# Retention and a normed two-layer block on one core: the norm's gain folded into w1, x of tiles 8 on normalized by ScalarE, and two more units of the first product built from seven half-size products

## The chip, the cores and the metric

The kernel runs on one core of a Trainium2 chip. The metric is the device time of one execution in microseconds (us). TensorE is called PE here as in the profile's rows (PEld is its weight loads), VectorE DVE, ScalarE ACT, GpSimd POOL and SyncE SP. Three runs of the kernel before are given, and one more execution that was profiled.

## What is computed

Inputs q, k and v have the shape 4 x 8 x 768 x 64 (batch, heads, sequence, head width). For each head a decaying state runs along the sequence; then a norm over the 512 features, a product with w1 (512 x 2048), a maximum with zero, a product with w2 (2048 x 512), and the sum with the input of the norm:

```python
gamma = 1.0 - 2.0 ** (-5.0 - np.arange(H))
state = gamma * state + k[t] (x) v[t]            # for t = 0 .. 767, each batch and head
y[t]  = scale * q[t] @ state
x  = y as [4, 768, 512]
mu, var = mean and variance of x over its 512 features
xn = (x - mu) / np.sqrt(var + 1e-06) * g_ln
out = x + np.maximum(xn @ w_ch1, 0.0) @ w_ch2
```

## The kernel before

**Tiles.** The 4 x 768 positions are 24 tiles of 128: tiles 0 to 3 are the first of each batch, then come five of batch 0 (4 to 8), five of batch 1, and so on. Everything between the loads and the store of the result stays on chip, and the state is carried between tiles of a batch as a sum in the PSUM bank PD.

**The order is written out by hand.** The string ORDER (lines 31 to 99) is a list of tokens. The loop at its end (lines 787 to 790) emits them one after the other, so an engine works through its own instructions in the order of the tokens, and an engine that waits for one token holds back all its later ones. A token is a name with numbers, then the engine where there is a choice (A is ACT, D DVE, S SP), then the PSUM banks that it uses (X0 to X3, Y0, Y1, M, PD). With the tile t the tokens are:

- `k`, `q`, `v` load a tile (line 355), issued by POOL; `gk`, `gq`, `gv` are POOL's waits for a landed load's buffer (line 384); `vg` is POOL's product of v with decay factors (line 475). `tr` transposes q and k of a tile from 7 on by a DMA issued by SP (line 398), `eq` scales q on DVE (line 404).
- `vis` (lines 407 to 422) is a visit of one tile, from tile 8 on of a pair of tiles: products of k and q into X banks, and the state's part of y into the banks Y0 and Y1. `am` is the mask on DVE (line 426), `py` adds the rest of y in Y0 and Y1 (line 441), `pd` adds to the state's sum in PD (line 483), and `pb` writes the next state out of PD, with ACT (line 494, four instructions) or DVE (line 498, two).
- Of a finished y: `bn` (lines 449 and 450, DVE) has mean and variance, `xc` (line 465, ACT) keeps x as bf16 for the end. `xn` (line 459, DVE) is (y - mean) times g; the row g is spread over the partitions by a matmul into `gb`. Up to tile 9 `xn` goes straight to the bf16 tile xn, and the factor 1/sqrt(var) is left to the end: `sq` and `rs` make it for a group, and `ad` (line 566, DVE) multiplies the second product by it and adds x. From tile 10 on (S0) `xn` goes to a float32 buffer (arg or grow), `sr` (line 577, ACT, square root) and `rt` (line 581, DVE, reciprocal) make the factor for the tile, and `xg` (line 585, ACT) multiplies by it into the bf16 tile. From tile 7 on y lies in Y0 and Y1 by halves (even and odd heads), so `xn` and `xc` come as a and b.
- `ex` brings xn transposed into xnt; from tile 8 (TX) on that is a DMA issued by SP (line 518).
- `m` (line 543) is a unit of the first product: 16 matmuls of 128 columns for a tile, or 8 of 256 columns for a group of two tiles, or 4 of 512 columns for a group of four; `r` (line 554 ACT or 556 DVE) takes the maximum with zero into h1. Tiles 0 to 7 are groups of one, 8 to 15 groups of two (groups 8 to 11), 16 to 19 and 20 to 23 groups of four (12 and 13).
- Six of the eight units of groups 12 and 13 (`seven` in line 18) use seven products of half the size in place of eight: `f` (line 646) has 4 matmuls of 256 columns; `fs` (line 657, ACT) copies a partial product out, `fo` (line 667, DVE) and `fq` (line 672, ACT) form the blocks of h1, `fr` (line 681 ACT or 679 DVE) takes the maximum with zero. `wm` (line 613, and 608 for number 3) and `xt` (line 629) make the sums of weights and of x, on DVE.
- `z` (line 561) is the second product up to tile 9. From tile 10 on it too goes by seven half-size products for a pair of tiles: `sa` (line 695, DVE) sums, `s` (line 706) 8 matmuls of 256 columns, `o` (line 720, DVE) additions that end in the output tile; `tm` (line 595) makes the sums of w2. `st` (line 573) stores, issued by ACT.

A visit writes Y0 and Y1, so it can't write y before `bn`, `xn` and `xc` of the visit before have read them.

Of the kernel before, what the change touches and what calls it, by code (L numbers as in the profile page):

```python
# [17 lines left out]
 'seven': [(12, 2), (12, 3), (13, 0), (13, 1), (13, 2), (13, 3)],  # L18
# [46 lines left out]
gq18 xg14 v19 rt15 vis16//X0,X1,X2,X3 ad9 st4/A ex14/S gq16 pd17 vg3/ am17a s10_1//M pb18/A am16a
tr18 m10_14//X2 v18 sa10_2 st7/A m10_12//X0 gk19 am16b v20 st5/A am17b pd3 gq19 m10_4//X1 tm3 pb19/A
tr19 py16 py17 m10_0//X3 sa10_4 r10_4/A xg15 bn17 m10_6//X1 xc16a ex15/S xc16b bn16 s10_5 r10_14/A
gv18 v21 xc17a tr20 sr17 s10_2//X2 xn17b r10_0/A gv19 rt17 k21 xn16a sr16 r10_6/A m10_2//X3 xn17a
o10_1 xc17b gk20 vg19/ xg17 m10_10//X1 rt16 o10_2 r10_12/A ex17/S q21 r10_2/A s10_6 eq18 xn16b
r10_10/A sa10_3 v22 s10_3 st6/A eq19 vis18//X0,X1,X2,X3 o10_3 o10_4 pd19 am19a s10_7 pb20/A gk21  # L70
am18a m10_8//X2 q22 o10_5 am18b s10_4 k22 r10_8/A am19b xg16 py18 sa12_1 q23 py19 st8/A m11_14//X0
ex16/S o10_6 gv20 bn19 vg20/ m11_2//X1 tr21 bn18 sr19 gq21 s12_1//M vg21/ xc19a xc19b wm1 m11_4//X2
sr18 vg22/ r11_14/A xc18a m11_6//X3 xc18b rt18 k23 xn19a r11_2/A rt19 s12_5 xn19b r11_6/A v23 xn18b
xg19 xn18a m11_10//X0 sa12_2 r11_4/A ex19/S xg18 pd20 o12_1 m11_0//X1 pb21/A wm2 ex18/S s12_2//X2
r11_0/A eq20 m11_8//X3 tr22 r11_10/A o12_2 eq21 s12_6 r11_8/A sa12_4 vis20//X0,X1,X2,X3 sa12_3 pd21
s12_3 am21a pb22/A am20b m11_12//X2 am21b m12_9//X1 am20a wm4 py20 r12_9/A py21 m12_0//X0 bn20
m12_1//X1 r12_0/A bn21 r11_12/A pd22 m12_10//X0 xc20a r12_1/A o12_3 m12_3//X2 pb23/A xn20a tr23
xt12_1 o12_4 m12_11//X1 xn21b sr20 xn21a xc20b s12_7 rt20 sr21 sa14_1 xc21a r12_10/A m12_2//X3 rt21
xn20b r12_3/A eq22 s14_1//PD o12_5 r12_2/A eq23 r12_11/A s12_4 wm3 xc21b st12/A vis22//X0,X1,X2,X3
st10/A xg21 xt12_2 s14_5 o12_6 xg20 am23b ex20/S f12_3_1//M am22a m12_8//X3 am22b st9/A ex21/S  # L80
fs12_3_1 f12_3_2//X0 am23a st11/A f12_3_5//X1 sa14_2 f12_3_6 fs12_3_5 fo12_3_1 f12_2_1//X2 r12_8/A
py22 xt12_3 f12_3_3 fs12_2_1 xt12_4 f12_2_5//X0 fs12_3_2 o14_1 f12_2_6 fs12_2_5 sa14_4 f12_3_7
fs12_2_2 py23 fo12_3_2 f12_2_3 f12_2_7 fo12_3_3 fr12_3_1/A s14_6 bn23 f13_1_1//X1 xc23b fo12_2_3
f12_3_4 xc22a f12_2_2//X3 fo12_2_2 fq12_3 f12_2_4 fo12_2_1 xc23a s14_2//X0 sr23 fq12_2 xn23b
fr12_2_1/A bn22 f13_1_2//X3 s14_3 fr12_2_2/A xn23a f13_0_1//X2 rt23 sr22 sa16_1 xc22b s16_1//M xg23
xn22a fr12_3_2/A rt22 ex23/S xn22b s16_5 o14_3 xg22 sa14_3 f13_0_2//Y0 ex22/S o14_4 s16_2//Y1 sa16_2
s14_7 o16_1 o14_2 s16_6 o14_5 st14/A sa16_4 fs13_0_1 s14_4 fs13_1_1 o16_2 sa16_3 f13_3_1//X0
f13_2_1//Y1 xt13_1 o14_6 s16_3 xt13_2 fo13_1_1 f13_0_5//PD fo13_0_1 f13_1_6 fs13_0_5 f13_0_6 sa18_1
fs13_3_1 f13_3_5//X3 xt13_3 fs13_1_2 f13_1_5//Y0 o16_3 fs13_0_2 f13_0_3 sa18_2 st15/A f13_3_6
fo13_0_2 fs13_2_1 f13_0_7 fs13_1_5 f13_1_7 o16_4 f13_2_6 fr13_0_1/A fo13_1_3 f13_3_2//PD xt13_4  # L90
s16_7 fs13_2_2 fo13_0_3 st13/A f13_1_3 fo13_3_1 f13_2_7 fo13_1_2 f13_1_4 fr13_1_2/D s18_1//PD
fs13_3_2 o16_5 fs13_3_5 f13_0_4 fq13_1 f13_3_7 fq13_0 f13_3_3 fo13_3_3 f13_2_5//X1 fo13_3_2
f13_2_2//X2 fs13_2_5 s18_5 sa18_4 fr13_3_1/A fo13_2_3 f13_3_4 f13_2_3 fr13_3_2/D fo13_2_1 s16_4
# [9 lines left out]
def kernel(  # L103
# [10 lines left out]
    nc = tc.nc  # L114
# [87 lines left out]
    xhat = [arg.rearrange("p i t -> p (i t)"), grow]  # L202
# [253 lines left out]
    @on("xn")  # L456
    def _(eng, t, half):
        dst, src, g = y_parts(t, half, slot(xns if t < S0 else xhat, t))
        nc.vector.scalar_tensor_tensor(out=dst, in0=src, scalar=mv[:, t, 0:1], in1=g,  # L459
                                       op0=ALU.subtract, op1=ALU.mult)  # L460
# [117 lines left out]

    @on("rt")
    def _(eng, t):  # L580
        nc.vector.reciprocal(out=rstd[:, t:t + 1], in_=rstd[:, t:t + 1])

    @on("xg")
    def _(eng, t):
        nc.scalar.activation(out=slot(xns, t), in_=slot(xhat, t), func=AF.Copy, scale=rstd[:, t:t + 1])
# [235 lines left out]
```

## Time and profile before

| | us |
|---|---|
| median of three runs | 206.64 (206.2 to 208.77) |
| the profiled execution | 205.83 |
| span from its first to its last instruction | 204.1 |
| PE, PEld busy | 195.7, 153.7 |
| DVE, ACT, POOL busy | 164.9, 103.0, 98.2 |

Granted TensorE clock: 0.996 over the span. The span leaves 1.7 us of the profiled execution outside. A row that groups instructions gives line, engine, operation, tiles written and read, shapes and count, then the time in which at least one of them ran and the mean duration of one; as neighbours overlap, the first divided by the count is less than the mean.

### The profile page before, as it was taken

To read this page: it belongs to the slowest core of one execution; us is meant where nothing else is said; L and a number is where in the kernel's file an instruction comes from. 1 tells how busy PE (TensorE), PEld (TensorE's weight loads), DVE (VectorE), ACT (ScalarE), POOL (GpSimd) and SP (SyncE) were. 2 spreads that over 40 slices of the span, in tenths; PEclk is the share of its full clock that TensorE was granted. 3 is DMA by queue.
4 is the path that set the end of the run, shared out by engine and by line. 5 is a ranking of instruction groups with operands and counts; after the bars stand their busy time and mean duration, and the time that the engine had idled before them with its cause. 6 is when DMAs were issued, how large, how long until landed. Compare 5 with 4: busy or idle time off the path is not lost.

```text
span 204.1 us, 5621 instructions
## 1 busy us (share of the span) xinstructions
PE 195.7 (96%) x2255; PEld 153.7 (75%) x2255; DVE 164.9 (81%) x380; ACT 103.0 (50%) x241; POOL 98.2 (48%) x145
## 2 busy tenths in 40 slices
PE   7988999999999999999999999999999999999992
PEld 2548899898645766668586988876579888888881
DVE  6677889769247879689398989999999899789871
ACT  5363654551331815926557684773967854641000
POOL 8986786496397599667298355960000000000000
PEclk9999999999999999999999999999999999999998
DMA  9999999999999999999999999999052031102025
GB/s 129 168 183 179 158 194 169 149 169 170 139 136 168 135 142 134 137 160 152 172 156 145 207 185 172 163 111 145 3 184 78 0 103 51 55 0 106 0 104 206
DMA packets 109949, 27.14 MB, mean 133 GB/s; under 512 B 102626, under 2 KB 106978, under 8 KB 109923
## 3 DMA queue, kind: packets, MB, share of 16 engines
q0 software_dynamic: 77024, 13.37, 92.7%
q1 hardware_dynamic: 28242, 6.85, 24.9%
q10 hardware_dynamic: 4656, 6.56, 10.5%
q8 instruction: 17, 0.28, 0.6%
q14 instruction: 10, 0.07, 0.1%
HBM read 27.30 MB, written 6.29 MB: 165 GB/s over the span
## 4 chain that ended last, share of the span: by engine, by line
PE 51%; DMA 27%; POOL 12%; issue 6%; DVE 2%; ACT 1%; POOLq 0%; ACTq 0%
PE X L543 16%; DMA v<-in_v_dram 11%; PE X L646 6%; DMA qk<-in_k_dram 6%; PE Y L706 6%; PE PD L706 5%; DMA qk<-in_q_dram 5%; DMA w<-in_moe_w_ch_dram 5%; PE M L706 4%; POOL qk L355 4%; PE Y L561 3%; POOL vg L475 2%; POOL scrap L384 2%; PE M L561 2%; PE X L706 2%
## 5 line engine op out<-in xcount | busy, mean ns | idle before, releaser
L543 PE MATMUL X<-xnt,w 128*128 128x128 bf16 (+2 forms) x800 | 71.2, 243 | 0.6 <-DMA w<-in_moe_w_ch_dram 0.6
L543 PEld LDWEIGHTS <-w 128*128 128x128 bf16 x800 | 56.9, 98 | 8.3 <-DMA w<-in_moe_w_ch_dram 0.8
L554 ACT ACTIVATE h<-X 128x512 bf16<-128x512 f32 x65 | 37.6, 609 | 22.7 <-PE X L543 22.6
L426 DVE TENSOR_TENSOR asb<-X,mask 128x512 bf16<-128x512 f32 x48 | 30.3, 682 | 5.9 <-PE X L413 5.7
L561 PE MATMUL M<-w,h 128*128 128x512 bf16 x128 | 30.8, 379 | 0.1
L561 PEld LDWEIGHTS <-h 128*128 128x128 bf16 x160 | 14.9, 98 | 14.6
L706 PEld LDWEIGHTS <-h 128*128 128x128 bf16 x224 | 21.8, 98 | 2.9
L475 POOL TENSOR_TENSOR vg<-v,vsc 128x512 bf16<-128x512 bf16 x16 | 17.7, 1106 | 9.7 <-DMA v<-in_v_dram 9.6
L494 ACT ACTIVATE state<-PD,gch 128x128 bf16<-128x128 f32 x44 | 12.6, 376 | 17.7 <-PE PD L483 17.7
L465 ACT CAST x_all<-Y 128x256 bf16<-128x256 f32 (+1 forms) x39 | 15.4, 408 | 9.9 <-DVE xn L459 7.8
L355 POOL DMA_DIRECT2D v<-in_v_dram x20 | 18.0, 903 | 3.4 <-DMA w<-in_moe_w_ch_dram 2.6
L449 DVE BATCH_NORM_STATS2 bns<-Y 128x6 f32<-128x256 f32 (+1 forms) x39 | 16.1, 450 | 4.3 <-PE Y L441 4.1
L706 PEld LDWEIGHTS <-sum 128*128 128x128 bf16 x168 | 16.3, 98 | 1.9
L355 POOL DMA_DIRECT2D qk<-in_q_dram x17 | 15.2, 893 | 1.3 <-issue 1.3
L355 POOL DMA_DIRECT2D qk<-in_k_dram x17 | 15.2, 898 | 0.9 <-issue 0.8
L695 DVE TENSOR_TENSOR sum<-h,sum 128x1024 bf16<-128x1024 bf16 x14 | 11.0, 784 | 0.1
L646 PEld LDWEIGHTS <-qk 128*128 128x128 bf16 x96 | 9.3, 98 | 1.0
L384 POOL COPY scrap<-qk 1x1 bf16<-1x1 bf16 x28 | 5.9, 212 | 8.5 <-DMA qk<-in_k_dram 6.9
L667 DVE TENSOR_TENSOR h<-X,tr 128x512 bf16<-128x512 f32 x12 | 8.0, 682 | 2.3 <-PE X L646 2.3
L566 DVE SCALAR_TENSOR_TENSOR osb<-M,rstd,x_all 128x512 f32<-128x512 f32 x8 | 6.0, 746 | 4.8 <-PE M L561 4.8
L657 ACT COPY tr<-X 128x512 f32<-128x512 f32 x12 | 6.6, 593 | 6.0 <-PE PD L706 2.4
L441 PEld LDWEIGHTS <-asb 128*128 128x128 bf16 x192 | 7.9, 98 | 2.0 <-DVE asb L426 0.8
(153 smaller groups left out, 342.8 us busy)
## 6 DMA issues: line engine op xcount, KB each, us to landing
out_dram<-osb ACTq DMA_DIRECT2D x23, 256.0 KB, 2.7
w<-in_moe_w_ch_dram POOLq DMA_DIRECT2D x8, 512.0 KB, 9.2
v<-in_v_dram POOLq DMA_DIRECT2D x20, 128.0 KB, 6.5
qk<-in_k_dram POOLq DMA_DIRECT2D x17, 128.0 KB, 5.9
qk<-in_q_dram POOLq DMA_DIRECT2D x17, 128.0 KB, 5.4
early<-in_q_dram POOLq DMA_DIRECT2D x6, 128.0 KB, 7.9
mid<-in_k_dram POOLq DMA_DIRECT2D x3, 128.0 KB, 8.2
mid<-in_v_dram POOLq DMA_DIRECT2D x3, 128.0 KB, 8.8
```

Of the source, the lines that this page charges most:

```text
L355: nc.gpsimd.dma_start(out=dst, in_=tok[kind][TILES[t]])
L426: nc.vector.tensor_tensor(out=slot(asb, t)[:, :, par, :], in0=bank(("pa", t, par)).rearrange("p (i t) -> p i t", t=P), in1=mask.rearrange( ...
L449: nc.vector.bn_stats(out=bns[:, t, i, :], in_=x)
L465: nc.scalar.copy(out=dst, in_=src)
L475: nc.gpsimd.tensor_tensor(out=slot(vgs, chunk(t)), in0=v_of(t), in1=vsc[:, c, :].unsqueeze(2).to_broadcast([P, H, D]), op=ALU.mult)
L494: nc.scalar.activation(out=slot(state, chunk(t) - 1)[:, i, :], in_=pd[:, i, :], func=AF.Copy, scale=gch[:, c - 1, i:i + 1])
L543: nc.tensor.matmul(bank(("mm", g, ho))[:, j * n * P:(j + 1) * n * P], lhsT=w1[:, ko, (ho + j) * P:(ho + j + 1) * P], rhs=x[:, x0:x0 + n, k ...
L554: nc.scalar.activation(out=dst, in_=src, func=AF.Relu)
L561: nc.tensor.matmul(bank(("m2", t)), lhsT=slot(h1, t // 4)[:, ho, t % 4 * P:(t % 4 + 1) * P], rhs=w2[:, ho, :], start=(ho == 0), stop=(ho = ...
L646: nc.tensor.matmul(f_bank(g, j, i)[:, n * 2 * P:(n + 1) * 2 * P], lhsT=f_left(i, ko)[:, (2 * j + n) * P:(2 * j + n + 1) * P], rhs=f_right( ...
L695: {"P": nc.gpsimd, "": nc.vector}[eng].tensor_tensor(out=out, in0=in0, in1=in1, op=ALU.subtract)
L706: nc.tensor.matmul(product(t, i), lhsT=left(t, i)[:, ho, :], rhs=right[i][:, ho, :], start=(ho == 0 and i in (1, 2)), stop=(ho == HK - 1), ...
```

## The change

- `gcol` loads g a second time, by columns (a partition holds the four values that belong to its rows of w1). `wg0` to `wg3` multiply the four 512-column parts of w1 in place by it: parts 0 and 3 on ACT, 1 and 2 on DVE, four instructions each. Each comes in the order after the last `m` of tiles 0 to 7 that reads its part.
- For tiles 8 on, `xn` is gone. `nb` (DVE, one column) makes -mean/sqrt(var), and `xg` reads y straight from its PSUM bank by halves on ACT, with scale and bias from columns, into the bf16 tile. So all tiles from 8 on have their factor before the first product; tiles 8 and 9 get `sr` and `rt` in place of `sq8` and `rs8`, and their `ad` is a plain sum.
- The other two units of group 12 (j = 0 and 1) go by seven products: eight `m12` and eight `r12` are gone; 14 `f`, 6 `fs`, 6 `fo`, 2 `fq`, 4 `fr` come. The partial products lie in arg, grow and gb, or in x_all and tr; the sums of w1 numbers 3 and 4 lie in x_all.
- `pb13/A`, `pb16/A` for DVE and `pb11`, `pb14`, `pb20` on DVE for ACT; four of the `fr` from DVE to ACT, two the other way.
- The order is new from the token after `tr7` on. The order of POOL's tokens among themselves is the one before, token by token. The last token is now `st23a` (half a tile); it was `st19` (a whole one).

The code, and of the order the stretch from visit 8 to visit 10 and the end:

```diff
 CFG = {'T0': 7,
- 'seven': [(12, 2), (12, 3), (13, 0), (13, 1), (13, 2), (13, 3)],
...
-z2_3 ad0 tr10 gq10 z3_0//M v12 gk11 st0/A ad2 z3_1 tr11 eq8 q13 vis8//X2,X1,X3,X0 sq6 z3_2 am9a am9b
-z3_3 am8a py9 am8b pd9 m6_4//X0 pb10/A ad3 gv10 vg10/ py8 m7_8//X1 bn8 gv11 q12 xc8a pd10 r6_4/A
-m7_12//X2 bn9 sq7 z4_0//M xn8b r7_12/A gk12 xn8a k13 pb11/A z4_1 eq10 ex8/S xn9b z4_2 xn9a xc8b xc9b
-ex9/S r7_8/A z4_3 eq11 xc9a gv12 q14 vis10//X0,X1,X2,X3 ad4 gq11 k15 am10a z5_0//M k14 am10b z5_1
+z2_3 ad0 tr10 gq10 z3_0//M v12 gk11 st0/A ad2 z3_1 tr11 eq8 q13 vis8//X2,X1,X3,X0 z3_2 am8a am8b
+z3_3 am9a pd9 ad3 py8 m7_8//X1 xc8a wg0/A gv10 vg10/ bn8 z4_0//M gv11 am9b z4_1 q12 eq10 r7_8/A py9
+z4_2 pb10/A bn9 gk12 z4_3 k13 sr8 sr9 rt8 xc9a nb8 pd10 rt9 m7_12//X0 nb9 ad4 xg9b xc9b xg8b z5_0//M
+eq11 xg8a xc8b gv12 pb11 ex8/S q14 r7_12/A z5_1 xg9a tm1 gq11 k15 vis10//X0,X1,X2,X3 ex9/S z5_2 k14
...
-o20_6 st21/A s18_4 st22/A o22_6 st23b/A st23a/A o18_6 st19/A
+s18_4 o22_4 o20_5 s22_7 o22_2 o18_2 o18_6 s20_4 st18/A o22_5 st19/A st22/A s22_4 o20_6 st23b/A
+st21/A o22_6 st23a/A
...
+    @on("gcol")
+    def _(eng):
+        nc.sync.dma_start(out=gcol, in_=moe_g_ln.rearrange("(ko p) -> p ko", p=P))
...
     def _(eng, t, half):
-        dst, src, g = y_parts(t, half, slot(xns if t < S0 else xhat, t))
+        dst, src, g = y_parts(t, half, slot(xns, t))
...
+        if t >= TX:
+            nc.vector.tensor_tensor(out=osb_of(t), in0=bank(("m2", t)), in1=x_all[:, t, :], op=ALU.add)
+            return
...
+    @on("nb")
+    def _(eng, t):
+        nc.vector.scalar_tensor_tensor(out=shift[:, t:t + 1], in0=mv[:, t, 0:1], scalar=-1.0,
+                                       in1=rstd[:, t:t + 1], op0=ALU.mult, op1=ALU.mult)
...
     @on("xg")
-    def _(eng, t):
-        nc.scalar.activation(out=slot(xns, t), in_=slot(xhat, t), func=AF.Copy, scale=rstd[:, t:t + 1])
+    def _(eng, t, half):
+        nc.scalar.activation(out=heads(slot(xns, t))[:, :, half], in_=split(y_of(t, half)),
+                             func=AF.Identity, bias=shift[:, t:t + 1], scale=rstd[:, t:t + 1])
+
+    @on("wg")
+    def _(eng, j):
+        for ko in range(KO):
+            w, g = w1[:, ko, j * DM:(j + 1) * DM], gcol[:, ko:ko + 1]
+            if eng == "A":
+                nc.scalar.activation(out=w, in_=w, func=AF.Copy, scale=g)
+            else:
+                nc.vector.tensor_scalar(out=w, in0=w, scalar1=g, scalar2=None, op0=ALU.mult)
...
     @on("wm")
     def _(eng, i):
-        if i == 3:
-            for ko in range(KH):
-                nc.vector.tensor_tensor(out=V3[ko], in0=block(1, 0)[:, ko], in1=block(0, 0)[:, ko],
-                                        op=ALU.subtract)
-            return
         out, in0, in1 = {1: (V1, block(1, 0), block(1, 1)), 2: (V2, block(0, 0), V1),
-                         4: (V4, block(0, 1), V2)}[i]
+                         3: (V3, block(1, 0), block(0, 0)), 4: (V4, block(0, 1), V2)}[i]
...
     @on("f")
     def _(eng, g, j, i):
-        for n in range(2):
+        nb, w = 8 // GROUPS[g], GROUPS[g] // 2 * P
+        for n in range(nb):
             for ko in range(KH):
-                nc.tensor.matmul(f_bank(g, j, i)[:, n * 2 * P:(n + 1) * 2 * P],
-                                 lhsT=f_left(i, ko)[:, (2 * j + n) * P:(2 * j + n + 1) * P],
+                nc.tensor.matmul(f_bank(g, j, i)[:, n * w:(n + 1) * w],
+                                 lhsT=f_left(i, ko)[:, (nb * j + n) * P:(nb * j + n + 1) * P],
                                  rhs=f_right(g, i)[:, :, ko, :], start=(n == ko == 0 and i in (1, 2, 5)),
                                  stop=(ko == KH - 1), skip_group_check=True)
```

The code for `f` and its sums is written for groups of two tiles too, but the order uses it for groups 12 and 13 alone; there a matmul of `f` still has 256 columns.

More of the change, by code (lines that the diff above doesn't have):

```diff
@@ L71 @@
[L71 to L81, printed above, removed]
@@ new lines @@
+eq20 s10_7 k22 r10_2/A rt19 bn18 r10_14/A m11_6//X0 q23 o10_5 sr18 m11_14//X2 gv20 rt18 tr21 nb19
+vg20/ sa12_1 xg19a xc18b nb18 s10_4 xg19b wm2 st7/A gq21 vg21/ ex19/S r11_14/A m11_0//X3 xg18a o10_6
+xg18b vg22/ pb20 xc18a s12_1//M ex18/S r11_8/A k23 sa12_2 pd20 s12_5 wm4 ex16/S pb21/A v23 s12_2//X1
+xc19a sa12_4 r11_0/A m11_12//X2 o12_1 xc19b r11_6/A pd21 o12_2 s12_6 r11_12/A eq21 pb22/A sa12_3
+vis20//X0,X1,X2,X3 xt12_3 s12_3 tr22 am21a am21b pd22 m11_4//X2 am20a py21 xt12_1 r11_4/A
+f12_1_1//X0 am20b m11_10//X3 xc21a xc21b xt12_2 fs12_1_1 bn21 f12_0_1//X1 r11_10/A f12_0_5//X2 tr23
@@ L168 @@
     gb = sb.tile([P, DM], FP32, name="gb")
+    gcol = sb.tile([P, KO], FP32, name="gcol")
     bns = sb.tile([P, NT, 2, 6], FP32, name="bns")
@@ L171 @@
     rstd = sb.tile([P, NT], FP32, name="rstd")
+    shift = sb.tile([P, NT], FP32, name="shift")
     touch = sb.tile([P, KO, 16], FP32, name="touch")
@@ L659, in h_block @@
     def h_block(g, j, half, n):
-        o = half * HK + 2 * j
-        return slot(h1, G0[g] // 4)[:, o:o + 2, n * 2 * P:(n + 1) * 2 * P]
+        nb, w, h0 = 8 // GROUPS[g], GROUPS[g] // 2 * P, G0[g] % 4 * P
+        o = half * HK + nb * j
+        if n is None:
+            return slot(h1, G0[g] // 4)[:, o:o + nb, h0:h0 + 2 * w]
+        return slot(h1, G0[g] // 4)[:, o:o + nb, h0 + n * w:h0 + (n + 1) * w]
     @on("fo")
@@ L671, in _ @@
     def _(eng, g, j):
-        nc.scalar.activation(out=h_block(g, j, 1, 0), in_=f_bank(g, j, 4).rearrange("p (j t) -> p j t", j=2),
+        nc.scalar.activation(out=h_block(g, j, 1, 0), in_=f_bank(g, j, 4).rearrange("p (j t) -> p j t", j=8 // GROUPS[g]),
                              func=AF.Relu)
@@ L676, in _ @@
     def _(eng, g, j, i):
-        h = slot(h1, G0[g] // 4)[:, 2 * j:2 * j + 2, :] if i == 1 else h_block(g, j, 1, 1)
+        h = h_block(g, j, 0, None) if i == 1 else h_block(g, j, 1, 1)
         if eng == "D":
@@ L757, in parse @@
             at(("py", int(arg)))
-        if kind in ("xn", "xc", "am", "st"):
+        if kind in ("xn", "xc", "xg", "am", "st"):
             m = re.fullmatch(r"(\d+)([ab]?)", arg)
```

113 lines of the change are left out of this document (62 added, 51 removed).

## The prediction

> **What bounds the kernel now.** I read the page's busy table first, then the windows, PE's waits, the chain, the groups kept apart by form, and last the timeline at two places. The page:
>
> ```profile
> span 204.1 us, 5621 instructions
> PE 195.7 (96%) x2255; PEld 153.7 (75%) x2255; DVE 164.9 (81%) x380; ACT 103.0 (50%) x241; POOL 98.2 (48%) x145
> ```
>
> PE stands out, but its ends are modelled, so the 96% alone proves little. The windows (us, then the busy time and count of PE, PEld, DVE, ACT, POOL) say where it is idle:
>
> ```profile
> 60.00:80.00 20.00, 19.94 (x242) 13.09 (x241) 16.20 (x34) 7.36 (x25) 16.40 (x28) 1.00 2.05 146
> 80.00:100.00 20.00, 20.00 (x184) 13.50 (x184) 14.38 (x36) 12.96 (x33) 12.86 (x22) 1.00 1.89 155
> 100.00:120.00 20.00, 20.00 (x243) 16.07 (x243) 18.35 (x44) 12.71 (x34) 11.78 (x19) 1.00 1.57 166
> 120.00:140.00 20.00, 19.48 (x242) 17.02 (x241) 18.94 (x38) 12.72 (x33) 13.51 (x18) 1.00 1.72 157
> 140.00:160.00 20.00, 20.00 (x203) 14.69 (x202) 19.10 (x44) 13.74 (x31) 0.00 (x0) 1.00 0.32 86
> 160.00:180.00 20.00, 20.00 (x186) 17.93 (x184) 17.73 (x41) 12.38 (x25) 0.00 (x0) 1.00 0.17 53
> 180.00:200.00 20.00, 20.00 (x185) 17.78 (x182) 17.18 (x37) 2.66 (x4) 0.00 (x0) 1.00 0.16 59
> ```
>
> From 60 to 200 us PE is idle for 0.06 + 0.52 = 0.58 us. DVE is close behind it from 100 to 160 (56.4 of 60 us), ACT never. Of what PE waited for, the largest that isn't all in the start-up (us in total, times, longest):
>
> ```profile
> PE X L413 <- DVE trq L404: 0.9, 4, 0.4
> ```
>
> The chain (start, us) shows whether the busy PE is a full PE, by runs of one kind:
>
> ```profile
> 127.97 4.75 DMA qk<-in_q_dram
> 132.72 2.08 DVE sum L695
> ...
> 152.06 0.86 PE X L543 x4
> 152.92 0.87 PE X L646 x8
> ...
> 195.75 3.49 PE Y L706 x32
> ```
>
> A matmul of 512 columns (an m12) takes 0.86/4 = 0.215 us, one of 256 columns (an f) 0.87/8 = 0.109, as also in a run of 32 (3.49/32). Half the width is half the time. Up to 132 us the chain also runs through loads, so the last visits get their data just in time; behind it is PE to the end. So a gain must be PE work taken away, or one of the few waits, or the tail.
>
> **The change part by part.**
>
> *PE work.* Eight m12 units of 4 matmuls go: 32 x 0.215 = 6.88 us. Fourteen f of 4 matmuls come: 56 x 0.109 = 6.10. PE loses **0.78 us**, all of it behind the last loads, where nothing but PE sets the pace. Every other matmul is the same and only moved. [...]
>
> *The engines beside it.* Rows by form (busy time, mean ns of one):
>
> ```profile
> L459 DVE SCALAR_TENSOR_TENSOR arg<-Y,mv,gb 128x256 f32<-128x256 f32 x14 | 6.5, 473 | 0.0
> L459 DVE SCALAR_TENSOR_TENSOR grow<-Y,mv,gb 128x256 f32<-128x256 f32 x14 | 6.4, 463 | 0.1
> L585 ACT ACTIVATE xn<-grow,rstd 128x512 bf16<-128x512 f32 x7 | 5.2, 749 | 0.7 <-DVE grow L459 0.7
> L465 ACT CAST x_all<-Y 128x256 bf16<-128x256 f32 x34 | 12.4, 382 | 7.3 <-DVE xn L459 5.1 <-DVE bns L449 1.3 <-DVE grow L459 0.4
> L494 ACT ACTIVATE state<-PD,gch 128x128 bf16<-128x128 f32 x44 | 12.6, 376 | 17.7 <-PE PD L483 17.7
> L554 ACT ACTIVATE h<-X 128x512 bf16<-128x512 f32 x65 | 37.6, 609 | 22.7 <-PE X L543 22.6
> L657 ACT COPY tr<-X 128x512 f32<-128x512 f32 x12 | 6.6, 593 | 6.0 <-PE PD L706 2.4 <-DVE h L667 1.8 <-PE X L646 1.8
> L667 DVE TENSOR_TENSOR h<-X,tr 128x512 bf16<-128x512 f32 x12 | 8.0, 682 | 2.3 <-PE X L646 2.3
> L679 DVE TENSOR_SCALAR h<-h 128x512 bf16<-128x512 bf16 x4 | 1.1, 284 | 0.0
> L681 ACT ACTIVATE h<-h 128x512 bf16<-128x512 bf16 x2 | 1.3, 636 | 0.0
> L681 ACT ACTIVATE h<-h 128x1024 bf16<-128x1024 bf16 x4 | 4.2, 1062 | 0.0
> L577 ACT ACTIVATE rstd<-mv,epsb 128x1 f32<-128x1 f32 x14 | 4.4, 312 | 2.6 <-DVE mv L450 2.6
> L581 DVE RECIPROCAL rstd<-rstd 128x1 f32<-128x1 f32 x14 | 2.0, 152 | 0.0
> ```
>
> DVE: 32 halves of xn go at 12.9/28 = 0.46, -14.7. Six fo come at 0.67, +4.0. wg1 and wg2 are eight instructions like L679; with a column as factor they may cost from 0.28 to twice that, I take the row, +2.2. nb is one column, like L581 (0.14) up to twice that, 16 of them, +2.3 at most. One pb more: +0.8. In all some 159 us against 164.9.
>
> ACT: 14 xg of 5.2/7 = 0.74 go, -10.4; 32 halves come. Their shape and source is that of L465 (0.365 of busy time each), and they have a scale and a bias from columns. L494, half as wide as L465 and with one such column, has a mean of 376 to its 382. So a half lies between 0.365 and the whole row's 0.74; I take 0.47, near the row of its own shape, +15.0 (11.7 to 23.7). wg0 and wg3: eight at 0.64 (0.58 of L554 to 0.74 of L585), +5.1. Eight r12 go, -4.6; fs, fq come, +3.3 and +1.2; four fr more and those from DVE, +4.1; one pb less, -1.1. In all some 116 us against 103.0, 57%.
>
> None of this is PE's, so it counts at nothing as long as PE has other work queued: DVE's relief of 6 us is worth at most the waits that DVE causes, 0.9 us, and ACT's 13 us are hidden by its idle half. Two places decide if they stay so.
>
> *Visit 10.* Here wg0 stands in ACT's queue ahead of r7_8, pb10 and the normalizing, and visit 10 can't write y before ACT has read Y0 and Y1. PE's prices at the visit before:
>
> ```profile
> 62.90 0.62 PE L413 MATMUL X<-trq,tr 64*128 64x128 bf16 x16
> 63.36 0.40 PE L419 MATMUL Y<-state,trq 64*128 64x64 bf16 x16
> 63.69 1.90 PE L561 MATMUL M<-w,h 128*128 128x512 bf16 x8
> 65.42 0.40 PE L441 MATMUL Y<-v,asb 128*128 128x64 bf16 x8
> 65.66 0.39 PE L483 MATMUL PD<-vg,qk 128*128 128x128 bf16 x4
> 65.88 1.06 PE L543 MATMUL X<-xnt,w 128*128 128x128 bf16 x16
> 66.77 0.40 PE L441 MATMUL Y<-v,asb 128*128 128x64 bf16 x8
> ```
>
> By starts: first part of a visit 0.46, py 0.24, pd 0.22, m of one tile 0.89, z 4 x 0.215 = 0.86. Between py8 and visit 10's first write of y the new order gives PE m7_8, z4_0 to z4_3, py9, pd10, m7_12, z5_0, z5_1 and that first part: 0.89 + 3.44 + 0.24 + 0.22 + 0.89 + 1.72 + 0.46 = 7.9 us. In the same stretch ACT has four xc (1.5), wg0 (2.6), two r (1.2), pb10 (4 x 0.29 = 1.1), two sr (0.6) and four xg (1.9): 8.9 us, or less where they follow closely. So ACT is late by up to 1.0 us, 0 at best; behind it queue PE's whole stream and with it all else. On DVE rt8 and nb8 wait for sr8, which stands behind wg0 too, and ad4 is queued behind them, which frees M for z5_0: the same lateness met a little earlier, not a second one. I take **+0.4**; with xg at its upper end it would be 2.0.
>
> *Visit 20.* PE waits for eq on DVE 0.9 us in all, and 0.52 of its idle time lies between 120 and 140, where this visit stands. The new order puts tr21, eq21 and the sums of the products in the same neighbourhood, with PE there some 0.7 us earlier in its work and with POOL's loads in the same order. DVE has sa12_4 and wm4 ahead of eq21 where it had the xn of two tiles. I take the old wait, a change of **0** (-0.7 to +0.8).
>
> *g by columns.* Its nearest row is another small load by SP, and the stores' rows serve for the tail:
>
> ```profile
> out_dram<-osb ACTq DMA_DIRECT2D x23, 256.0 KB, 2.7
> out_dram<-osb ACTq DMA_DIRECT2D x2, 128.0 KB, 2.2
> touch<-in_moe_w_ch_dram SPq DMA_DIRECT2D x1, 32.0 KB, 4.8
> ```
>
> gcol is issued behind tr7, and wg0 wants it behind py8, with visits 6, 7 and 8 between them: their work covers 4.8 us, without which wg0 and ACT's queue behind it would be late by that. On SP it stands ahead of tr9, whose loads k9 and q9 come later in the order. **0.** The chain now ends with a store of half a tile in place of a whole one, 2.2 for 2.7: **-0.2** (0 to -0.5), as the stores ahead of it share the engines.
>
> *Sum:* -0.78 + 0.4 + 0 + 0 - 0.2 = -0.6 us, a span of 203.5 and, against this execution's own 205.83, 205.2. That execution lies 0.4 under the fastest of the three runs (206.2) and 0.8 under their median; I add the smaller offset: **205.6**. Its own bounds (-0.78 with -0.7, 0 and -0.5, or with +2.0 and +0.8) give 203.9 to 208.2, nearly all below 207.
>
> **The rivals.**
>
> 1. *The normalizing on ACT paces every visit* (slower). y used to be read by DVE and ACT side by side; now ACT reads it eight times a visit, behind r, pb and wg in its one queue, and only after sr, rt and nb. For: L465's idle time shows that y's readers wait for each other already, and ACT's load grows just where PE fills X banks that wait for r. Against: ACT is idle over a third of the time there, and elsewhere no wg stands in its queue next to a visit's last readers but wg3. It passes 2% once a visit loses over 0.65 us on average; at 0.75 in all eight it adds 6.0: 211.6. Chance 0.12, of which 0.09 is over 2%.
> 2. *The waits go too* (faster). DVE's relief lifts PE's waits for eq and visit 10 has none: -0.78 - 0.9 - 0.2, and with an estimated 0.7 of gaps that the modelled ends may hide, 203.6. For: 19.10 of 20 us of DVE between 140 and 160. Against: PE is idle for 0.58 us only behind 60. Chance 0.09, with 0.03 for more than 2%.
> 3. *The loads set visit 20 whatever PE does*, and the new order does less behind them: the 0.78 is given back as a longer wait, 206.4. For: the chain up to 132 us. Against: the loads are as before and the saved work lies behind them. Chance 0.07.
> 4. *The seven products save nothing.* From 6.88/56 = 0.123 us on for a matmul of f there is no gain; at 0.137, a quarter over the row, the 56 cost 7.7, which turns -0.78 into +0.8: 207.2. For: with more matmuls come more weight loads, and PEld is at 17.9 of 20 us from 160 to 180. Against: just there f and s keep 0.109. Chance 0.02. [...]
>
> The forecast has 0.70. A measurement of this kernel can tell about 2%, 4.1 us, from no change: under 202.5 only the rest of rival 2 and a little of the forecast, **0.04**; over 210.8 rival 1, **0.10**; within, **0.86**. The range leaves out the worse half of rival 1: **203.2 to 208.8**.
>
> **What would show it.** Right: PE has 2255 - 32 + 56 = 2279 matmuls; L646's runs keep 0.109; DVE falls by about 6 us and ACT rises by about 13; PE's waits behind 60 us stay near 1 us in all, with a new one at visit 10. Wrong: PE waits at the y part of several visits with ACT's xg as releaser, windows of PE under 19 us between 60 and 160, or xg with a mean over 0.6 us.

## The result, and the profile after

The changed kernel takes 209.21 us (median of 16 runs, 206.81 to 211.2) where the kernel before takes 207.67 (16 runs, 205.3 to 212.75): a ratio of 1.0101, 95% interval 1.0064 to 1.0139. Forecast was a gain of 0.6 us, with 208.8 as the upper end. Ratios and intervals leave disturbed runs out and medians count every run, so the two can differ: for the kernel before on the chip of e1 to e4 the median is 208.41 of all runs and 206.1 of the undisturbed ones. The profiled execution took 209.05, 3.2 more than that of before, and its span grew by the same 3.2. The page, in the lines that answer to those of before:

```profile
span 207.3 us, 5696 instructions
PE 197.3 (95%) x2279; PEld 157.6 (76%) x2279; DVE 164.0 (79%) x379; ACT 115.5 (56%) x269; POOL 96.6 (47%) x145
```

PE has the 2279 matmuls that were forecast and ACT the forecast 116 us. DVE has not fallen by 6 us, only by 0.9. The windows of the changed kernel:

```profile
80.00:100.00 20.00, 18.72 (x205) 12.68 (x204) 16.08 (x39) 16.84 (x44) 11.63 (x23) 1.00 1.65 166
...
120.00:140.00 20.00, 17.80 (x190) 15.12 (x188) 16.74 (x33) 9.91 (x27) 11.72 (x17) 0.91 1.49 132
140.00:160.00 20.00, 20.00 (x258) 17.74 (x257) 19.27 (x48) 14.33 (x37) 0.00 (x0) 1.00 0.38 68
```

Two windows hold less than 19 us of PE, which the prediction had named as a sign against it, and both lie ahead of the place where the matmuls were saved. PE's waits name DVE, and not ACT:

```profile
PE M L736 <- DVE osb L750: 2.2, 2, 2.0
PE M L567 <- DVE osb L575: 1.3, 1, 1.3
```

**At 84 us** PE wants bank M for z7_0, and ad6 has not yet read it. DVE's timeline (start, us, what) shows what ad6 (L575) stands behind, and PE's the wait:

```profile
80.70 1.44 DVE L609 TENSOR_SCALAR w<-w,gcol 128x512 bf16<-128x512 bf16 x4
...
82.13 1.99 DVE L619 TENSOR_TENSOR early<-w,early 128x2048 bf16<-128x2048 bf16 x1
...
84.11 0.73 DVE L575 SCALAR_TENSOR_TENSOR osb<-M,rstd,x_all 128x512 f32<-128x512 f32 x1
```
```profile
84.89 1.89 PE L567 MATMUL M<-w,h 128*128 128x512 bf16 x8 [1.28 <-DVE osb L575]
```

Of that, 0.8 us is tm2 (L619), which takes 1.99 us here. POOL's product vg began first beside it:

```profile
81.86 1.18 POOL L481 TENSOR_TENSOR vg<-v,vsc 128x512 bf16<-128x512 bf16 x1 [0.46 <-DMA v<-in_v_dram]
```

In another execution of the same kernel (e12 below) tm2 began first. There tm2 took 1.20 us and vg the longer time, and PE waited 0.55 us in place of 1.28:

```profile
82.76 1.20 DVE L619 TENSOR_TENSOR early<-w,early 128x2048 bf16<-128x2048 bf16 x1
```
```profile
82.97 1.90 POOL L481 TENSOR_TENSOR vg<-v,vsc 128x512 bf16<-128x512 bf16 x1 [0.93 <-DMA v<-in_v_dram]
```

**At 122 us** DVE stands still although its input is ready (its releaser is "issue"): o10_1 overwrites the slot of osb from which the store st5 reads, and st5, issued at 113.6 us, has not landed. The view of the tile osb between 95 and 130 us gives the time from issue to landing of the stores in it:

```profile
121.99 0.69 DVE L750 TENSOR_TENSOR osb<-M,x_all 128x512 f32<-128x512 f32 x1 [2.79 <-issue]
...
DMA to landing us min/median/max: 3.8/3.9/8.3
```
```profile
122.73 1.69 PE L736 MATMUL M<-early,sum 128*128 128x256 bf16 x8 [1.96 <-DVE osb L750]
```

**From 126 to 136 us** the chain that ended last leaves PE and runs down DVE's queue (start, us, what):

```profile
126.10 1.28 DVE asb L432 x2
...
130.30 1.82 DVE trq L410
...
134.34 1.14 DVE qk L630
135.48 0.35 DVE osb L750
135.87 1.03 PE M L736 x8
```

In this execution the queue costs PE little: PE runs at half its clock up to 126.4 us, and from 124 to 141 us its only idle time is 0.24 us, ahead of 135.87. Other executions lose more there, as shown below. The odd piece is eq20: 1.82 us, where an eq takes 0.41. Here it is in the timelines of DVE and of POOL:

```profile
130.22 1.90 DVE L410 TENSOR_TENSOR trq<-tr,qsc 128x512 bf16<-128x512 bf16 x1
```
```profile
129.79 2.04 POOL L481 TENSOR_TENSOR vg<-v,vsc 128x512 bf16<-128x512 bf16 x2
```

It ends 0.3 us behind the end of POOL's two products vg. The trace of before has the same in it: a sum (sa12_2) beside the same two vg, 2.10 us where the other sums of its kind take 0.68, and with nothing urgent behind it. There eq20 came at 136.5 us and took 0.41.

```profile
132.69 2.10 DVE L695 TENSOR_TENSOR sum<-h,sum 128x1024 bf16<-128x1024 bf16 x1
```
```profile
132.22 2.03 POOL L475 TENSOR_TENSOR vg<-v,vsc 128x512 bf16<-128x512 bf16 x2
```

The first theory was the first two places, ad6 and the store; eq20 came in only when moving those two had not brought the time back. The rivals: that the two more units don't save on PE; that the normalizing on ACT costs it; that these waits belong to one execution only.

### The profile page after: what moved, and what is told of

Read it like the earlier page. It is cut to its first block, busy times and chain, and to the rows that moved or that the text cites. A ratio compares the mean times of both kernels' runs of the same rounds, so it can differ in the third digit from the quotient of the medians.

```text
span 207.3 us, 5696 instructions
## 1 busy us (share of the span) xinstructions
PE 197.3 (95%) x2279; PEld 157.6 (76%) x2279; DVE 164.0 (79%) x379; ACT 115.5 (56%) x269; POOL 96.6 (47%) x145
## 4 chain that ended last, share of the span: by engine, by line
PE 51%; DVE 7%; issue 1%; ACT 0%; DVEq 0%
PE M L736 12%; PE X L549 10%; PE X L670 8%; PE M L567 5%; PE Y L736 5%; PE X L736 3%; PE Y L670 2%; PE X L419 2%; PE PD L670 2%; PE Y L447 1%; DVE osb L750 1%; DVE asb L432 1%; DVE early L619 1%; PE PD L489 1%; DVE trq L410 1%
## 5 line engine op out<-in xcount | busy, mean ns | idle before, releaser
L549 PE MATMUL X<-xnt,w 128*128 128x128 bf16 (+1 forms) x768 | 63.6, 237 | 0.0
L549 PEld LDWEIGHTS <-w 128*128 128x128 bf16 x768 | 53.8, 98 | 4.6 <-issue 0.2
L560 ACT ACTIVATE h<-X 128x512 bf16<-128x512 f32 x57 | 33.5, 606 | 19.7 <-PE X L549 17.2
L471 ACT CAST x_all<-Y 128x256 bf16<-128x256 f32 (+1 forms) x39 | 15.6, 413 | 16.4 <-PE Y L447 8.4
L599 ACT ACTIVATE xn<-Y,shift,rstd 128x256 bf16<-128x256 f32 x32 | 18.1, 591 | 1.9 <-DVE shift L590 1.7
L736 PE MATMUL M<-early,sum 128*128 128x256 bf16 x80 | 11.0, 283 | 2.0 <-DVE osb L750 2.0
L586 ACT ACTIVATE rstd<-mv,epsb 128x1 f32<-128x1 f32 x16 | 4.6, 303 | 12.9 <-DVE mv L456 12.8
L410 DVE TENSOR_TENSOR trq<-tr,qsc 128x512 bf16<-128x512 bf16 x17 | 8.4, 500 | 3.8 <-DMA tr<-qk 3.8
L736 PE MATMUL M<-w,h 128*128 128x256 bf16 x80 | 10.4, 273 | 0.2 <-DVE osb L750 0.2
L750 DVE TENSOR_TENSOR osb<-M,x_all 128x256 f32<-128x256 f32 (+1 forms) x15 | 7.6, 505 | 3.5 <-issue 2.8
L756 PE MATMUL PD<-zeros 128*128 128x512 bf16 (+1 forms) x33 | 9.2, 417 | 1.2 <-DVE zeros L270 1.2
```

The costliest lines, as they stand in the source:

```text
L471: nc.scalar.copy(out=dst, in_=src)
L549: nc.tensor.matmul(bank(("mm", g, ho))[:, j * n * P:(j + 1) * n * P], lhsT=w1[:, ko, (ho + j) * P:(ho + j + 1) * P], rhs=x[:, x0:x0 + n, k ...
L560: nc.scalar.activation(out=dst, in_=src, func=AF.Relu)
L599: nc.scalar.activation(out=heads(slot(xns, t))[:, :, half], in_=split(y_of(t, half)), func=AF.Identity, bias=shift[:, t:t + 1], scale=rstd ...
L736: nc.tensor.matmul(product(t, i), lhsT=left(t, i)[:, ho, :], rhs=right[i][:, ho, :], start=(ho == 0 and i in (1, 2)), stop=(ho == HK - 1), ...
```

## The experiments

Each is an edit of the order (tokens) of one of the two kernels. Medians stand with that of the kernel before on the same chip.

### The store and ad6

**e1_store_early**

```diff
-nb17 st5/A bn16
+nb17 bn16
-st6/A am12b
+st6/A st5/A am12b
```

> The changed kernel with one token moved: the store of tile 5 is issued next to that of tile 6 at about 85 us and not at 113.6. Theory (late releases): PE's wait of 1.96 us at 121 us, where the sum o10_1 may not overwrite the output tile until that store has landed, goes, and with it the halved clock of 3.4 us behind it; the wait of 1.3 us at 83 us for ad6 stays. Some 2 to 3.3 us less than the changed kernel's 209.2, so 206 to 207, a ratio to the kernel before of about 0.995. Rival (the normalizing on ACT paces the visits): the store is not the cause, PE waits as long at the same place or the next, ratio still 1.01.

207.62 us (12 runs) beside 208.41; ratio 1.0117 (1.0065 to 1.0169). The wait for osb at 122 us is gone in the profile, but by the ratio the time is not nearer to before than the changed kernel's. eq20 takes 2.92 us here, and PE waits 0.84 and 0.53 us for osb at 132 and 134 us.

**e5_before_late_store**, the same in the kernel before:

```diff
-v20 st5/A am17b
+v20 am17b
-xg15 bn17
+xg15 st5/A bn17
```

> The kernel before with one token moved: the store of tile 5 is issued some 4 to 5 us later, behind the normalizing of tile 15. Theory (a late store of tile 5 holds the first sum of tile 10, and that the products behind it): a wait of PE for DVE's osb of 1 to 4 us appears near 120 to 124 us, and with a wait near 2 us a halved clock behind it; ratio 1.005 to 1.025. Rival (the wait in the changed kernel comes from ACT's normalizing and the store only lies beside it): no wait, ratio 1.00.

207.92 beside 206.93; ratio 1.0095 (1.0025 to 1.0164), with a wait of 1.52 us for osb at 122.9. A late store alone makes this wait in another order.

**e2_ad6_first**, **e3_both** (with st5 as in e1) and **e7_three** (e3 with o10_6 from behind xg18a to behind s10_4):

```diff
-rs6 v15 tm2
+rs6 ad6 v15 tm2
-rt11 ad6 r8_2/A
+rt11 r8_2/A
```

> The changed kernel with one token moved: the sum ad6 stands on DVE ahead of tm2 and of rt11 in place of behind them. Theory: the wait of z7_0 for bank M at 83.4 to 84.9 us goes, 1.3 us; the wait at 121 us stays. 207.9, ratio about 1.004. Rival (ACT paces the visits): visit 12 waits for the normalizing of tiles 10 and 11 in its place and the time stays at 209.2.

> Both moves in one kernel. Theory: both waits go, PE ends some 3.3 us earlier and 4.7 us with the clock, so 204.5 to 206 where the kernel before is at 207.7 on the whole, ratio 0.985 to 0.992. Rival (ACT paces the visits): the waits come back elsewhere, ratio 1.005 or more.

> Both moves, and the sum o10_6 ahead of wm2 on DVE, for which PE waited 0.24 us (a gap of 0.4) at 135.5 us. Theory: 0.3 to 0.4 us less than with both moves. Rival: nothing, since DVE is busy there in any order.

e2: 209.37 beside 208.41, ratio 1.0131 (1.0027 to 1.0234). e3: 208.02 beside 208.41, ratio 1.0107 (1.0017 to 1.0197). e7: 208.82 beside 206.93, ratio 1.014 (1.0082 to 1.0199). None of them is back at the kernel before: with ad6 ahead PE comes earlier to part 3 of w1, which ACT's wg3 has to finish first, and waits 0.33 us for it at 88 to 90 us; from 131 to 137 us it still waits 0.5 to 1.8 us. In e7 ad6 came late all the same (0.85 us). The theory of two places did not hold; something at 130 us was missing from it.

### Parts of the change undone or doubled

**e4_m12**: `f12_0` and `f12_1` with their fs, fo, fq and fr are the eight m12 and r12 of before again. **e6_no_wg** leaves out wg0 to wg3, and so the gain for the tiles from 8 on. **e8_xg_twice** emits every xg twice.

> The changed kernel with the two added units of group 12 undone: eight units of four matmuls of 512 columns with eight evacuations on ACT, in the places of the half-size products. Theory: PE has 32 x 0.215 in place of 56 x 0.109 us, 0.78 us more, and both waits stay: 210.0, 0.8 more than the changed kernel, if DVE and ACT don't pace that stretch. Rival (the half-size products load DVE, which paces the stretch from 140 us on): undoing them costs nothing or gains up to 1 us.

> The changed kernel without the sixteen products of w1 with g: the gain is left out for tiles 8 on. Theory: DVE is 2.9 us earlier at ad6, so the wait of 1.3 us at 83 us goes, and the 0.3 at 70.8 us before visit 10 nearly; the wait at 121 us for the store stays. 207.6, ratio about 1.003. Rival (the reading of y by ACT paces the visits, wg or not): 209.2 and the same waits.

> The changed kernel with each normalizing instruction on ACT given twice (the same result written twice), which puts 32 x 0.45 = 14 us more on ACT. Theory (ACT has room, the waits are DVE's and the store's): under 2 us more than 209.2, ratio under 1.02. Rival (ACT paces the visits): most of the 1.8 us a visit shows, 8 us or more, ratio 1.05.

e4: 210.58 beside 208.41, ratio 1.0217 (1.0123 to 1.0312), which shows no loss by the two units; its profiled execution has a wait of 3.1 us at 124, so the ratio doesn't weigh their 0.78 us. e6: 206.39 beside 206.93, ratio 1.0014 (0.9943 to 1.0086): without the eight instructions on DVE and the eight on ACT the waits at 71 and 84 us are gone. In its profiled execution, the longest of its four, eq20 still takes 3.14 us and PE waits 1.28 and 0.53 us behind it, so eq20 is not the only thing that decides whether the time is level. e8: 227.24 beside 206.93, ratio 1.1051 (1.0974 to 1.1128). That is far over the theory's 2%, and on the rival's side (8 us or more). 32 more halves, one every 0.45 us (81.03, 81.48 in the changed kernel), are 14 us of ACT's work and cost 18. ACT's 56% are no cover for a doubled xg; its r, which free the X banks, are queued behind it:

```profile
PE X L421 <- ACT h L562: 5.3, 5, 2.2
```

The changed kernel itself has no such wait in its list.

### eq20 beside POOL

Four kernels on one chip, kernel before 206.86 (23 runs). **e10_eq20**:

```diff
-eq20 s10_7
+s10_7
-o12_2 s12_6
+o12_2 eq20 s12_6
```

**e9_store_eq20** has st5 moved too; **e11_all** has st5, ad6, eq20 and o10_6 moved, and wg3 from behind vg14 to behind r7_12; **e12_after_again** is the changed kernel.

> The changed kernel with eq20 alone moved to behind o12_2. Theory: eq20 takes 0.41 to 0.5 us; the wait for osb at 121 to 123 us (the late store st5) stays at 1 to 2 us since nothing of it is touched; the small wait at 136 us goes. Gain against the changed kernel 0 to 0.6 us. Rival (the order of VectorE as a whole is what costs): no gain, and a wait as large elsewhere between 128 and 140 us.

> The changed kernel with two tokens moved: the store st5 behind st6, and eq20 (VectorE multiplies q of tile 20 by its decay) from ahead of rt19 to behind o12_2, shortly ahead of eq21. Theory: in the changed order eq20 stands beside GpSimd's vg20 to vg22 and takes 1.7 to 2.9 us in place of 0.41, and everything behind it on VectorE (rt19, bn18, o10_5, wm2, o10_6) is late; that is the TensorE wait of about 1.7 us at 131 to 135 us that stayed when st5 alone was moved. Moved late, eq20 takes 0.41 to 0.5 us, the waits between 129 and 137 us fall under 0.6 us in sum, and the time is 1.0 to 1.5 us under that of the kernel with st5 alone moved, 2 to 3 us under the changed kernel run beside it. Rival: the queue of VectorE is simply too long there, and whichever instruction with two inputs in SBUF comes next beside GpSimd is stretched in its place; then the wait stays within 0.4 us and the time is that of st5 alone.

> The changed kernel with five tokens moved: st5 behind st6, ad6 ahead of tm2 (behind rs6), eq20 behind o12_2, wg3 (ScalarE's 2.5 us of the gain into part 3 of w1) early, into ScalarE's idle time before r7_4, and o10_6 ahead of wm2. Theory: with the waits found so far taken away (1.3 for ad6, 2.0 for the store with 1.4 of clock behind it, 0.7 for wg3, about 1 for eq20), the 0.78 us saved on TensorE shows: a span of 203 to 204.5, 1.5 to 4 us under the changed kernel and 0 to 1.5 under the kernel before. Rival: with these gone, the next waits come up (state, xg, osb) and the time stays at 207 or above, no better than before.

> The changed kernel as it is, beside the three others on the same chip. Theory: 0.5 to 1.5% over the kernel before, with the waits at 83 to 85 us (1.3) and at 121 to 123 us (about 2) again. Rival: the waits are those of one execution; another execution has other ones, and the ratio is under 0.5%.

| | us | ratio, interval |
|---|---|---|
| e12, changed | 209.08 | 1.0138 (1.0088 to 1.0188) |
| e10, eq20 late | 206.86 | 1.0017 (0.9976 to 1.0058) |
| e9, eq20 late, st5 early | 206.96 | 1.0031 (0.9989 to 1.0073) |
| e11, all five | 209.99 | 1.0141 (1.0068 to 1.0214) |

The changed kernel repeats its loss; its profiled execution here, the fastest of its six (207.19), has the waits at 85 and 121 us at 0.55 and 0.48 us, and eq20 at 1.89 again, so the size of the first two differs between executions. One token takes 2.2 us off, more than the 0 to 0.6 that was expected, and moving the store as well adds nothing to it. PE's timeline from the visit of tile 18 to that of tile 20, in e12 and in e10:

```profile
122.13 0.62 PE L419 MATMUL X<-trq,tr 64*128 64x128 bf16 x16
...
133.99 1.03 PE L736 MATMUL M<-w,h 128*128 128x256 bf16 x8 [0.53 <-DVE osb L750]
...
138.90 0.62 PE L419 MATMUL X<-trq,tr 64*128 64x128 bf16 x16
```
```profile
124.33 0.62 PE L419 MATMUL X<-trq,tr 64*128 64x128 bf16 x16
...
139.48 0.74 PE L419 MATMUL X<-trq,tr 64*128 64x128 bf16 x16
```

The work of PE in it is the same, and the clock is full in both. From one visit to the next go 16.8 us in e12 and 15.2 in e10: late DVE instructions cost e12 1.6 us here, in three waits (0.24 for asb, 0.29 and 0.53 for osb by the view, each some 0.17 more from start to start). In the first profile of the changed kernel it is 16.4 us, of which 0.9 is the halved clock and 0.4 the wait at 135.87. The kernel before has 14.5 us, but its order gives PE a unit of eight matmuls and a pd less in this stretch, 1.1 us of work.

In e10 the vg pair stands beside norms and o10_5, and eq20 shares 0.75 us with eq21 later:

```profile
130.35 0.76 DVE L455 BATCH_NORM_STATS2 bns<-Y 128x6 f32<-128x256 f32 x2 [0.28 <-PE Y L447]
...
131.28 0.41 DVE L750 TENSOR_TENSOR osb<-M,osb 128x256 f32<-128x256 f32 x1
...
138.91 0.75 DVE L410 TENSOR_TENSOR trq<-tr,qsc 128x512 bf16<-128x512 bf16 x2
```
```profile
130.29 2.03 POOL L481 TENSOR_TENSOR vg<-v,vsc 128x512 bf16<-128x512 bf16 x2
```

e11 undid the gain: with wg3 in ACT's queue early, the xg ahead of visit 10 are late and PE waits 2.3 us for them, the cost that the prediction had feared of wg0. So ACT's idle time there was not free.

**e14_before_eq20** puts eq20 beside POOL in the kernel before; **e15_vg_late** takes POOL's vg21 and vg22 away from it in the changed one.

```diff
-r11_0/A eq20 m11_8//X3
+r11_0/A m11_8//X3
-k23 xn19a
+k23 eq20 xn19a
```
```diff
-gq21 vg21/ ex19/S
+gq21 ex19/S
-xg18b vg22/ pb20
+xg18b pb20
-v23 s12_2//X1
+v23 vg21/ vg22/ s12_2//X1
```

> The kernel before with eq20 alone moved early, to behind k23 and so ahead of xn19a: on VectorE it then comes up at about 131 us, beside GpSimd's vg20 to vg22. Theory: eq20 takes 1.5 to 3.3 us in place of 0.41, whatever the order around it, and sa12_2 (2.10 us in the profile of before) falls to about 0.7; the time rises by 0 to 1.5 us, as far as xn19 and bank copies behind it are waited for. Rival: eq20 was slow only by what the changed order puts around it (another buffer, the transposing DMA of q): then it takes 0.41 us here and the time stays.

> The changed kernel with VectorE's order untouched; on GpSimd vg21 and vg22 are moved behind the loads k23 and v23, so that eq20 no longer stands beside them. Theory (two inputs in SBUF on VectorE wait out GpSimd's multiplication): eq20 takes 0.41 to 1.0 us where it is, and a later instruction (a sum or wm2, at 132 to 135 us) is stretched to over 1.5 us in place of it; the time falls by 0.5 to 2 us against the changed kernel if that one has less behind it, and stays if not. Rival (eq20 is slow for its input, tr of tile 20, or by the loads): it takes 1.7 to 3.1 us again.

e14: 209.05 beside 207.29, ratio 1.0144 (1.0081 to 1.0207): a loss as large as that of the change, out of one moved token, and more than the 0 to 1.5 us that were expected. DVE, POOL and ACT in e14:

```profile
131.38 3.45 DVE L404 TENSOR_TENSOR trq<-tr,qsc 128x512 bf16<-128x512 bf16 x1
```
```profile
131.39 1.03 POOL L475 TENSOR_TENSOR vg<-v,vsc 128x512 bf16<-128x512 bf16 x1
...
132.52 2.03 POOL L475 TENSOR_TENSOR vg<-v,vsc 128x512 bf16<-128x512 bf16 x2
```
```profile
135.72 0.72 ACT L585 ACTIVATE xn<-grow,rstd 128x512 bf16<-128x512 f32 x1 [2.98 <-DVE grow L459]
```

eq20 waits out all three vg, xn19 behind it is late, ACT waits for xn19, and PE waits 2.0 us for the r that is queued behind that. e15: 209.17 beside 207.29, ratio 1.0134 (1.0072 to 1.0196): no gain. eq20 still takes 1.56 us, not the 0.41 to 1.0 expected, beside vg20 and the load issued behind it, and two nb behind it, of one column each, take 0.56 and 0.99 in place of 0.15. The stretch went to other instructions of the same queue. In it the block also went the other way: the vg pair takes 2.59 us, 0.56 more than elsewhere, with a sum of 0.68 us that DVE ran in that time at its usual length:

```profile
132.29 0.68 DVE L725 TENSOR_TENSOR sum<-h 128x1024 bf16<-128x1024 bf16 x1
132.89 0.99 DVE L590 SCALAR_TENSOR_TENSOR shift<-mv,rstd 128x1 f32<-128x1 f32 x1
```
```profile
131.27 2.59 POOL L481 TENSOR_TENSOR vg<-v,vsc 128x512 bf16<-128x512 bf16 x2
```

The rows have one thing in common. What took longer beside vg has two inputs in SBUF: eq20 (0.41 us elsewhere, 1.56 to 3.45 beside it), a sum (0.68, and 2.10 in before), tm2 (1.20, and 1.99) and nb (0.15, and up to 0.99 in e15). In e10 the o10_5 with one input in PSUM and the norms, which read PSUM, keep their 0.41 and 0.76 beside the same vg pair. Why the two kinds differ no run shows. One more thing stays open: in e15 eq20 ends 1.0 us behind vg20, while POOL only issues a load; in e10 a sum that stands beside such an issue at 132.3 us keeps its 0.68.

### What was left

**e13_store_ad6_eq20**, **e16_wg3_dve** (e13 with `wg3/D` for `wg3/A`), then on another chip **e17_tm2_late** beside **e18_store_eq20_again** (e9 once more). e17 is e9 with:

```diff
-v15 tm2 xc11a
+v15 xc11a
-ad7 q17
+ad7 tm2 q17
```

> The changed kernel with three tokens moved: st5 behind st6, ad6 ahead of tm2 (behind rs6), eq20 behind o12_2. Theory: the three waits (1.3 at 84 us, up to 2.0 at 122, about 1.6 between the visits of tiles 18 and 20) are the whole of the loss; with all three gone the saving on TensorE shows, less the 0.7 us by which part 3 of w1 is then waited for at 88 us: 0.5 to 1.5 us under the kernel before. Rival: moving ad6 gains nothing, since the next thing in that stretch (part 3 of w1, scaled by ScalarE) is late by as much; the time is that of st5 and eq20 moved, equal to the kernel before within 0.5 us.

> The changed kernel with st5, ad6 and eq20 moved, and wg3 given to VectorE (four of 0.36 us in place of ScalarE's four of 0.64). Theory: the TensorE wait of 0.7 us for part 3 of w1 at 88 us goes as well, and ScalarE is 2.5 us less behind there: 0.3 to 1 us under the kernel with three tokens moved, 1 to 2 us under the kernel before. Rival: VectorE is as full there (state and four asb follow), and the products with asb behind visit 12 are late by what wg3 takes, 0.4 to 1.4 us: no gain.

> The changed kernel with st5 behind st6, eq20 behind o12_2, and tm2 (VectorE, 1.2 to 2.0 us) from ahead of rt11 to behind ad7, into 3.07 us in which VectorE is idle; nothing is put ahead of ad6. Theory: the wait of 0.7 us for bank M at 85 us goes and nothing takes its place, since nothing but a later sum needs tm2; with the store and eq20 out of the way too, the saving on TensorE shows: 0.5 to 1.0 us under the kernel with st5 and eq20 moved, 0.5 to 1.5 us under the kernel before. Rival: TensorE catches up and then waits for the next late thing (the load of q for eq15 at 98 us, asb, osb); the time is that of st5 and eq20 moved, level with the kernel before.

> The changed kernel with st5 and eq20 moved, as run before, beside the kernel with tm2 moved as well on the same chip. Both theories: level with the kernel before within 0.7 us.

e13: 211.24 us beside 207.29, without a ratio; in its profile a sum (L725) stands beside the vg pair and takes 2.67 us, and PE waits 1.37 us for the asb behind it. It decides nothing. e16: 207.92 beside 207.29, ratio 1.0012 (0.9961 to 1.0062): level, with 1.7 us of waits for asb, as its rival said. e17: **205.57** beside 207.65, ratio 0.9956 (0.9913 to 1.0). e18: 206.86 beside 207.65, ratio 1.0015 (0.9969 to 1.006). e17 is 1.3 us under e18 by the medians, though their intervals overlap, and has the lowest median of all. tm2 moved into idle time of DVE leaves ad6 early, and z7_0 follows pd at once, in PE's timeline of e17:

```profile
83.69 0.39 PE L489 MATMUL PD<-vg,mid 128*128 128x128 bf16 x4
83.92 1.89 PE L567 MATMUL M<-w,h 128*128 128x512 bf16 x8
```

Behind 60 us no wait of PE in e17 is over 0.33 us (for part 3 of w1). PE is busy for 19.30 us of the window from 80 to 100 us and for 19.86 from 120 to 140, where the changed kernel has 18.72 and 17.80.

## Why the prediction was wrong, and where it was right

- **PE work, -0.78: right in kind.** There are 2279 matmuls, and f keeps 0.109 in the chain of the changed kernel (the row `155.55 0.87 PE X L670 x8`). With the late instructions out of the way e17 is 0.44% under before, some 0.9 us. That fits the saving, but the interval just reaches no change.
- **The failed step: "None of this is PE's, so it counts at nothing as long as PE has other work queued", and "Two places decide if they stay so".** There were more. I priced each moved instruction by a mean row, but eq20 took 0.41 us or 1.56 to 3.45 by what POOL did beside it. For visit 20 the prediction took "the old wait" and looked at tr21 and eq21; it was eq20, moved some 6 us earlier into POOL's vg, and the instructions queued behind it on DVE. Shown by e10 and e12 (2.2 us by the medians, 1.6 us from visit 18 to visit 20 in their profiles) and e14 (1.4% in the kernel before). It isn't a sum of separate losses: e6, with wg left out and eq20 in its place, is level with before too.
- **tm2 and ad6, not in the prediction.** wg1, wg2 and tm2 stand ahead of ad6. wg on DVE took 0.36 each (2.9 us for 2.2 forecast), and tm2 1.99 beside vg for the 1.19 it took before. Together they make ad6 late by the 1.28 us that PE waits, though DVE has idle time enough on average. e17 against e18: 1.3 us.
- **The stores' slots were not costed.** The change moves stores as well as o tokens. The wait of 1.96 us in the profiled execution is real, and e5 makes it in the kernel before; but beside a repaired eq20 its removal gained nothing measurable (e9, e10). Why PE gains nothing from the 1.5 us of that wait in e10 stays open.
- **Visit 10, +0.4: right in size, and nearly so in mechanism.** By the rows `69.65 1.06 PE L549`, `70.84` for z5_0 and `72.79` for visit 10, with 16 x 0.056 for the m and 8 x 0.215 for the z, PE is late by 0.30 and 0.23 us. The first is ad4 behind sr8 behind wg0, as said. The second is not yet the write of y: the visit's first part wants bank X0, and ACT's r7_12, queued behind its reading of Y, frees it at 72.74. With wg3 there too (e11) the write of y itself waits, 2.3 us.
- **ACT +13: right** (115.5 of 116), with xg above its price:

```profile
L599 ACT ACTIVATE xn<-Y,shift,rstd 128x256 bf16<-128x256 f32 x32 | 18.1, 591 | 1.9 <-DVE shift L590 1.7 <-ACT xn L599 0.2
```

  18.1/32 = 0.57 for 0.47 taken. Rival 1 did not come: PE has no wait for ACT's xg at the visits in the changed kernel. But that ACT's work is "hidden by its idle half" was luck of the order, as e8 and e11 show.
- **DVE -6: wrong, -0.9.** The 32 halves of xn went. They follow each other every 0.38 us (131.08 to 131.46 in before), so 32 of them free 12.2 us, and not the 14.7 of their busy rows; wg and nb (3.0 us) cost 1.4 more than their rows said, eq and tm came out longer by another 2.4, and the sums of h 1.5 shorter.
- **The tail, -0.2: did not come.** From the start of the last eight matmuls to the end of the span go 5.02 us before (199.08 to 204.1) and 5.16 after (202.14 to 207.3).
- **Rivals 2 to 4** did not come: the waits grew, visit 20 was not set by loads, and f costs what it should. The 0.7 us of hidden gaps in rival 2 was an estimate of mine that no run shows.
- **A slip of the working.** Of the sum's own bounds the upper one has the offset of 0.4 in it and the lower one hasn't: with it, 204.2 to 208.2. It does not change the forecast.

## What to carry to other kernels

Before an instruction is moved, look at what the other engine does at its new place: here DVE's instructions with two inputs in SBUF were the ones that took longer beside GpSimd's vg (eq20 1.56 to 3.45 us for 0.41, a sum 2.10 for 0.68), and eq20, put where no vg stood beside it, gained 2.2 us by the medians. An order written by hand is priced by its queues and not by busy time; for each moved instruction list what stands behind it on its engine, stores and buffer slots included. And one removed wait is not a gain until its neighbours are known: here ad6 put ahead of tm2 gained nothing, and tm2 put into idle time gained 1.3 us by the medians.

## What the runs showed of the hardware

- eq20, a 128x512 bf16 product on DVE, took 0.41 us with no vg beside it (before) and 1.56 (e15) to 3.45 (e14) beside GpSimd's vg; an nb, one column, took 0.15 with none beside it and 0.56 and 0.99 beside the vg pair in e15.
- Of the stores issued between 95 and 130 us in the changed kernel the middle one landed after 3.9 us and the slowest, st5, after 8.3.
- The granted clock fell to half behind the wait of 1.96 us, as in the windows of the changed kernel:

```profile
123.00:126.00 3.00, 3.00 (x42) 2.17 (x40) 2.19 (x4) 0.00 (x0) 1.12 (x3) 0.50 2.34 149
```

  It fell in e11 too behind 2.3 us (0.53 from 77 to 80 us) and in e4 behind 3.1 (0.67 from 125 to 128), but not in e14 behind 2.0 (1.00 from 136 to 146), so the length of the wait alone does not tell when. What else does, no run shows.
